# Two of five units' probabilities transposed by VectorE and GpSimd instead of TensorE, dense rows on 128 partitions, and a new order, in a two-layer recurrent-memory attention kernel

## Chip, cores, metric

One core of a Trainium2 chip runs the kernel. The metric is device microseconds of one execution, the median of three runs: 1588.75 us (1588.54 to 1590.98).

## What is computed

The input x has 2048 rows of 512. Two pairs of layers with shared weights follow each other: attention with a recurrent memory, then a dense layer, and both again.

```python
def _A_ref(x, mem0, Wq, Wk, Wv, Wo, seg_len):     # seg_len 32, M = 8 memory rows, 32 heads of 128
    mem = mem0
    for s in range(n_seg):                        # 64 segments
        h = jnp.concatenate([mem, xs], axis=1)    # 8 + 32 = 40 rows
        q, k, v = (einsum('btd,dhe->bhte', h, W) for W in (Wq, Wk, Wv))
        scores = jnp.where(mask, einsum(q, k) * scale, -1e9)
        o = einsum(softmax(scores), v)
        o = einsum('bhte,hed->btd', o, Wo)
        mem = o[:, :M, :]                         # goes into the next segment
        outs.append(o[:, M:, :])
...
x = x + _A_ref(_layernorm(x), ...)
x = x + relu(_layernorm(x) @ w1) @ w2             # 512 -> 1376 -> 512
x = x + _A_ref(_layernorm(x), ...)
x = x + relu(_layernorm(x) @ w1) @ w2
```

The memory rows make the segments of a layer a chain: segment s+1 needs the projected memory of segment s.

## The kernel before

**Steps.** Two layers run interleaved. Step k works on segment k of the first attention layer and on segment k-2 of the second (66 steps; in steps 2 to 63 both are there, "full steps"). Both segments lie side by side in HT: 2 x 40 columns, so most matmuls have 80 moving columns.

**Units.** The 32 heads form four groups p of eight. A unit is (p, xs): units 0, 1 and 2 hold eight heads each (groups 0, 1, 2), units 3 and 4 half of group 3 each. Per step and unit:

- queries_keys: 16 matmuls for four heads' q or k, copied from PSUM to qT and kT (L982 on ScalarE, L984 on VectorE).
- scores (L1133): small matmuls into one PSUM bank; rows of 40 queries at partitions 0 and 64.
- softmax: mask add (L1144), maximum (L1148), subtraction (L1151), exp on ScalarE (L1155), sum (L1158), reciprocal (L1161), multiply into P (L1175, on VectorE or GpSimd).
- turn: matmuls against the identity transpose P into PSUM (part of L726); two masked copies (L1198 on ScalarE, L1200 on VectorE) bring it to PT, one per block b of heads, with the other block's rows set to zero.
- attend (L1217): matmuls with PT as moving operand, eight per full unit, then a copy to OT.
- project: 16 matmuls for four heads (L726, st<-OT,Wo_sb), summed over all units in one PSUM bank. Project 0 is first, project 4 (16 matmuls) last. Then the memory columns go to the next step's HT.

Line 726 is the helper `across`, which issues most matmuls. Beside attention a step has the value matmuls (L1048), the dense layer of the step before, and, in steps 5 to 54, pieces of later values (vg).

**Dense layer (finish).** OX is transposed by a DMA to rows y, 64 rows of 512; add (L924), layernorm (L749, L752, L731 and L736 on GpSimd, L755), a TensorE turn of four blocks with 64 columns each ("turn da"), w1 and relu, w2 (L821), the total with x (L940, two halves), a second layernorm for the second attention layer, a turn of four blocks with 32 columns ("turn db"). GpSimd moves rows between x and Z (L909, L957, L962).

**Order.** A planner gives each engine its instructions in a fixed order. TensorE's order is a table: an operation in step k has the priority PERIOD * k + PLACE[name, phase], and TensorE takes them sorted.

```python
if PE in o.cost:
    o.prio = PERIOD * o.step + PLACE.get((o.key, phase(o.step)), -99.0)
...
first = [o for o in sorted(self.ops, key=lambda o: (o.prio, o.seq)) if PE in o.cost]
```

Phase 0 is the steady phase; phases 2 to 4 are steps 0, 1 and 2, phases 5 and 6 the last two. The other engines take what the planner's cost model has ready first, with AHEAD and the tables' priorities to choose among what is ready within LOOK. PAIRED names operations that may run as two matmuls of 64 output columns where TensorE is in that tile mode already. Buffers are rings: es has two, PT three.

Of the kernel before, what the change touches and what calls it, by code (L numbers as in the profile page):

```python
# [8 lines left out]
BF = mybir.dt.bfloat16  # L9
# [21 lines left out]
LOOK = 0.0763052  # L31
PERIOD = 26.155362
PLACE = {
    ("*turned.turng0.0", 2): -89.961, ("*turned.turng1.0", 2): -29.171, ("*turned.turng2.0", 2): -21.854,
    ("*turned.turng3.0", 2): -18.856, ("*turned.turng4.0", 2): 7.73, ("*turned.turng5.0", 2): 3.668,
    ("*turned.turng6.0", 2): 21.105, ("*turned.turng7.0", 2): 35.848, ("*values.mmg0.0", 2): -24.752,
    ("*values.mmg0.1", 2): -25.658, ("*values.mmg0.2", 2): -13.629, ("*values.mmg0.3", 2): -5.241,
    ("*values.mmg1.0", 2): -23.988, ("*values.mmg1.1", 2): -24.752, ("*values.mmg1.2", 2): -5.58,
    ("*values.mmg1.3", 2): -5.826, ("*values.mmg2.0", 2): -0.166, ("*values.mmg2.1", 2): -7.867,
    ("*values.mmg2.2", 2): -12.27, ("*values.mmg2.3", 2): -17.638, ("*values.mmg3.0", 2): -8.777,  # L40
    ("*values.mmg3.1", 2): 0.348, ("*values.mmg3.2", 2): -0.279, ("*values.mmg3.3", 2): 11.874,
    ("*values.mmg4.0", 2): 60.771, ("*values.mmg4.1", 2): 43.21, ("*values.mmg4.2", 2): 50.685,
    ("*values.mmg4.3", 2): 32.375, ("*values.mmg5.0", 2): 14.472, ("*values.mmg5.1", 2): 50.454,
    ("*values.mmg5.2", 2): 20.334, ("*values.mmg5.3", 2): 7.7, ("*values.mmg6.0", 2): 39.239,
    ("*values.mmg6.1", 2): 51.082, ("*values.mmg6.2", 2): 32.453, ("*values.mmg6.3", 2): 32.134,
    ("*values.mmg7.0", 2): 67.088, ("*values.mmg7.1", 2): 44.861, ("*values.mmg7.2", 2): 63.527,
    ("*values.mmg7.3", 2): 78.999, ("attend.mmu0.0", 0): 46.198, ("attend.mmu0.0", 2): 43.372,
    ("attend.mmu0.0", 3): 43.359, ("attend.mmu0.0", 4): 41.947, ("attend.mmu0.0", 5): 52.115,
    ("attend.mmu0.0", 6): 51.839, ("attend.mmu1.0", 0): 48.361, ("attend.mmu1.0", 2): 43.267,
    ("attend.mmu1.0", 3): 48.433, ("attend.mmu1.0", 4): 43.811, ("attend.mmu1.0", 5): 53.564,  # L50
    ("attend.mmu1.0", 6): 52.286, ("attend.mmu2.0", 0): 52.242, ("attend.mmu2.0", 2): 48.839,
    ("attend.mmu2.0", 3): 49.155, ("attend.mmu2.0", 4): 51.459, ("attend.mmu2.0", 5): 54.271,
    ("attend.mmu2.0", 6): 56.839, ("attend.mmu3.0", 0): 52.917, ("attend.mmu3.0", 2): 48.735,
    ("attend.mmu3.0", 3): 48.727, ("attend.mmu3.0", 4): 53.577, ("attend.mmu3.0", 5): 54.512,
    ("attend.mmu3.0", 6): 59.465, ("attend.mmu4.0", 0): 54.218, ("attend.mmu4.0", 2): 46.589,
    ("attend.mmu4.0", 3): 51.493, ("attend.mmu4.0", 4): 52.878, ("attend.mmu4.0", 5): 50.927,
    ("attend.mmu4.0", 6): 62.122, ("dense_layer.mm.da.0", 0): 69.095, ("dense_layer.mm.da.0", 2): 69.092,
    ("dense_layer.mm.da.0", 3): 71.014, ("dense_layer.mm.da.0", 4): 67.121, ("dense_layer.mm.da.0", 5): 78.081,
    ("dense_layer.mm.da.0", 6): 149.332, ("dense_layer.mm.da.1", 0): 69.149, ("dense_layer.mm.da.1", 2): 69.678,
    ("dense_layer.mm.da.1", 3): 72.44, ("dense_layer.mm.da.1", 4): 68.335, ("dense_layer.mm.da.1", 5): 81.881,  # L60
    ("dense_layer.mm.da.1", 6): 163.656, ("dense_layer.mm.da.2", 0): 69.921, ("dense_layer.mm.da.2", 2): 69.865,
    ("dense_layer.mm.da.2", 3): 72.468, ("dense_layer.mm.da.2", 4): 69.033, ("dense_layer.mm.da.2", 5): 78.483,
    ("dense_layer.mm.da.2", 6): 166.387, ("dense_layer.mm.da.3", 0): 72.962, ("dense_layer.mm.da.3", 2): 72.508,
    ("dense_layer.mm.da.3", 3): 75.407, ("dense_layer.mm.da.3", 4): 72.576, ("dense_layer.mm.da.3", 5): 91.676,
    ("dense_layer.mm.da.3", 6): 169.361, ("dense_layer.mm.da.4", 0): 74.146, ("dense_layer.mm.da.4", 2): 73.088,
    ("dense_layer.mm.da.4", 3): 75.634, ("dense_layer.mm.da.4", 4): 73.89, ("dense_layer.mm.da.4", 5): 96.131,
    ("dense_layer.mm.da.4", 6): 202.721, ("dense_layer.mm.da.5", 0): 74.607, ("dense_layer.mm.da.5", 2): 73.784,
    ("dense_layer.mm.da.5", 3): 76.032, ("dense_layer.mm.da.5", 4): 76.254, ("dense_layer.mm.da.5", 5): 117.834,
    ("dense_layer.mm.da.5", 6): 266.417, ("finish.turn_near.0", 6): 67.931, ("idle.spins.0", 6): 75.636,
    ("late_values.mmv0.0", 0): 55.822, ("late_values.mmv1.0", 0): 56.364, ("prepare.turns.0", 2): -92.733,  # L70
    ("project.mm.0", 0): 50.503, ("project.mm.0", 2): 48.522, ("project.mm.0", 3): 47.695,
    ("project.mm.0", 4): 46.462, ("project.mm.0", 5): 54.013, ("project.mm.0", 6): 55.445,
    ("project.mm.1", 0): 52.792, ("project.mm.1", 2): 48.552, ("project.mm.1", 3): 50.859,
    ("project.mm.1", 4): 53.188, ("project.mm.1", 5): 54.467, ("project.mm.1", 6): 56.904,
    ("project.mm.2", 0): 53.979, ("project.mm.2", 2): 51.927, ("project.mm.2", 3): 51.15,
    ("project.mm.2", 4): 54.567, ("project.mm.2", 5): 55.41, ("project.mm.2", 6): 61.468,
    ("project.mm.3", 0): 54.515, ("project.mm.3", 2): 52.343, ("project.mm.3", 3): 51.498,
    ("project.mm.3", 4): 54.73, ("project.mm.3", 5): 59.493, ("project.mm.3", 6): 62.385,
    ("project.mm.4", 0): 54.829, ("project.mm.4", 2): 52.707, ("project.mm.4", 3): 51.859,
    ("project.mm.4", 4): 55.104, ("project.mm.4", 5): 63.208, ("project.mm.4", 6): 63.808,  # L80
    ("queries_keys.mmu0.0", 0): 33.177, ("queries_keys.mmu0.0", 2): -2.267, ("queries_keys.mmu0.0", 3): 28.414,
    ("queries_keys.mmu0.0", 4): 30.223, ("queries_keys.mmu0.0", 5): 31.574, ("queries_keys.mmu0.0", 6): 40.535,
    ("queries_keys.mmu0.1", 0): 35.022, ("queries_keys.mmu0.1", 2): 10.309, ("queries_keys.mmu0.1", 3): 28.972,
    ("queries_keys.mmu0.1", 4): 29.109, ("queries_keys.mmu0.1", 5): 29.899, ("queries_keys.mmu0.1", 6): 38.292,
    ("queries_keys.mmu0.2", 0): 32.038, ("queries_keys.mmu0.2", 2): 5.691, ("queries_keys.mmu0.2", 3): 29.761,
    ("queries_keys.mmu0.2", 4): 27.054, ("queries_keys.mmu0.2", 5): 35.233, ("queries_keys.mmu0.2", 6): 41.032,
    ("queries_keys.mmu0.3", 0): 34.046, ("queries_keys.mmu0.3", 2): 8.234, ("queries_keys.mmu0.3", 3): 27.267,
    ("queries_keys.mmu0.3", 4): 27.106, ("queries_keys.mmu0.3", 5): 33.701, ("queries_keys.mmu0.3", 6): 40.622,
    ("queries_keys.mmu1.0", 0): 33.29, ("queries_keys.mmu1.0", 2): -3.555, ("queries_keys.mmu1.0", 3): 33.083,
    ("queries_keys.mmu1.0", 4): 30.633, ("queries_keys.mmu1.0", 5): 30.415, ("queries_keys.mmu1.0", 6): 41.01,  # L90
    ("queries_keys.mmu1.1", 0): 31.691, ("queries_keys.mmu1.1", 2): 7.644, ("queries_keys.mmu1.1", 3): 35.745,
    ("queries_keys.mmu1.1", 4): 27.445, ("queries_keys.mmu1.1", 5): 31.218, ("queries_keys.mmu1.1", 6): 42.927,
    ("queries_keys.mmu1.2", 0): 31.569, ("queries_keys.mmu1.2", 2): -4.781, ("queries_keys.mmu1.2", 3): 33.431,
    ("queries_keys.mmu1.2", 4): 31.298, ("queries_keys.mmu1.2", 5): 31.356, ("queries_keys.mmu1.2", 6): 40.49,
    ("queries_keys.mmu1.3", 0): 31.637, ("queries_keys.mmu1.3", 2): 9.921, ("queries_keys.mmu1.3", 3): 34.111,
    ("queries_keys.mmu1.3", 4): 29.304, ("queries_keys.mmu1.3", 5): 31.132, ("queries_keys.mmu1.3", 6): 44.867,
    ("queries_keys.mmu2.0", 0): 37.201, ("queries_keys.mmu2.0", 2): 26.988, ("queries_keys.mmu2.0", 3): 40.496,
    ("queries_keys.mmu2.0", 4): 36.639, ("queries_keys.mmu2.0", 5): 37.862, ("queries_keys.mmu2.0", 6): 46.536,
# [120 lines left out]


def t_dve(n, rate=1):
    return 0.07 + 1.042e-3 * n / rate


PART, MASKED = {ACT: 0.13, DVE: 0.10}, {ACT: 0.11, DVE: 0.065}
XBAR = 0.5, 0.2, 2.6


def t_pool(n):
    return 0.06 + 2.2e-3 * n  # L230


def t_copy(n):
    return 0.06 + 1.3e-3 * n


def phase(step):

# [1137 lines left out]
```

## Time and profile before

| what | us |
|---|---|
| median of three runs | 1588.75 |
| profiled execution, first to last instruction | 1588.6 |
| PE, PEld busy | 1569.5, 1411.1 |
| DVE, ACT, POOL busy | 1082.3, 1165.2, 314.3 |
| a full step, start to start | 23.35 to 23.8 |
| transposes of P on PE (L726, work<-ident,P), 756 of 128 and 536 of 64 output columns | 59.3 and 22.0 busy |
| masked copies to PT on ACT (320 and 160 elements) | 133.1 and 97.8 |
| masked copies to PT on DVE (320 elements) | 65.9 |

A line of the groups holds the source line, engine, operation, tiles written and read, shapes, the count, then busy time, mean time of one in ns, and the idle time ahead of it with what ended it. A line of the timeline holds the start, the length, engine, line, operation, tiles and the count that was merged. PEld is TensorE's weight load, which runs beside the matmuls; SPq is the sync engine's queue of DMA issues. The granted TensorE clock was 0.998 over the run.

### The profile page before, as it was taken

How to read it: one execution, taken by the hardware profiler on the slowest of the kernel's cores; microseconds unless marked ns; L12 is line 12 of the kernel's file. 1: busy time of each engine (PE TensorE's matmuls, PEld its weight loads, DVE VectorE, ACT ScalarE, POOL GpSimd, SP SyncE). 2: the span in 40 equal slices, each digit the busy share in tenths (PEclk: the TensorE clock that was granted, in tenths of full speed). 3: DMA queues.
4: the chain of work that ended last, by engine and by line, in shares of the span. 5: the costliest groups of instructions: out<-in, count | busy, mean ns of one | idle time of the engine just before them, and what ended most of it. 6: DMA issues, size and time to landing. Idle time of an engine off the chain costs nothing.

```text
span 1588.6 us, 100346 instructions
## 1 busy us (share of the span) xinstructions
PE 1569.5 (99%) x45458; PEld 1411.1 (89%) x45458; DVE 1082.3 (68%) x2957; ACT 1165.2 (73%) x3073; POOL 314.3 (20%) x667
## 2 busy tenths in 40 slices
PE   8999999999999999999999999999999999999998
PEld 5689999999999989999989999999998998898887
DVE  4566766766776776686676677677667667667665
ACT  4667777777777777777777777777777777777774
POOL 5112112212112212121121221211211121112110
PEclk9999999999999999999999999999999999999999
DMA  9711111111111111111111111111111111111100
GB/s 371 243 44 30 26 33 32 29 35 37 25 39 31 35 29 33 29 32 40 26 36 27 35 26 42 37 26 38 25 35 28 33 33 29 33 25 22 28 21 9
DMA packets 76540, 70.89 MB, mean 45 GB/s; under 512 B 50920, under 2 KB 62416, under 8 KB 76112
## 3 DMA queue, kind: packets, MB, share of 16 engines
q1 hardware_dynamic: 70096, 44.14, 13.1%
q0 software_dynamic: 4992, 19.40, 3.4%
q8 instruction: 356, 5.83, 1.6%
q10 hardware_dynamic: 1024, 0.93, 0.2%
q14 instruction: 72, 0.59, 0.1%
HBM read 31.53 MB, written 9.96 MB: 26 GB/s over the span
## 4 chain that ended last, share of the span: by engine, by line
PE 97%; DMA 1%; DVE 1%; POOL 1%; ACT 0%; issue 0%; DVEq 0%; POOLq 0%
PE work L726 40%; PE st L726 19%; PE fill L1048 16%; PE fill L726 8%; PE fill L821 5%; PE work L1217 5%; PE work L1133 4%; DMA xg<-in_A_x_dram 0%; DMA y<-OX 0%; DMA w_sb<-in_B_w_dram 0%; ACT HT L982 0%; POOL Wo_sb L537 0%; PE fill L711 0%; DVE ln L749 0%; POOL ln L736 0%
## 5 line engine op out<-in xcount | busy, mean ns | idle before, releaser
L726 PE MATMUL work<-HT,Wq_sb 128*128 128x80 bf16 (+2 forms) x10400 | 361.8, 201 | 3.1 <-ACT HT L982 3.1
L726 PE MATMUL work<-HT,Wk_sb 128*128 128x80 bf16 (+2 forms) x10416 | 362.7, 201 | 0.8 <-ACT HT L982 0.8
L726 PEld LDWEIGHTS <-Wq_sb 128*128 128x128 bf16 (+1 forms) x10400 | 330.9, 104 | 20.8 <-issue 6.0
L726 PE MATMUL st<-OT,Wo_sb 128*128 128x80 bf16 (+1 forms) x8448 | 345.5, 201 | 0.0
L726 PEld LDWEIGHTS <-Wk_sb 128*128 128x128 bf16 (+1 forms) x10416 | 327.1, 104 | 17.3 <-issue 2.0
L726 PEld LDWEIGHTS <-Wo_sb 128*128 128x128 bf16 x8448 | 315.7, 100 | 13.0 <-issue 12.7
L1048 PE MATMUL fill<-Wv_sb,HT 128*64 128x512 bf16 x2112 | 273.6, 381 | 1.1 <-DVE HT L984 1.0
L982 ACT CAST kT<-work 128x320 bf16<-128x320 f32 (+1 forms) x523 | 218.3, 418 | 68.6 <-PE work L726 31.1
L982 ACT CAST qT<-work 128x320 bf16<-128x320 f32 (+1 forms) x516 | 215.7, 418 | 67.5 <-PE work L726 47.2
L1198 ACT ACTIVATE PT<-work,half 128x160 bf16<-128x160 f32 (+1 forms) x515 | 231.3, 463 | 20.1 <-PE work L726 12.7
L982 ACT CAST OT<-work 128x320 bf16<-128x320 f32 (+1 forms) x461 | 186.2, 420 | 50.7 <-PE work L1217 50.6
L982 ACT CAST vw<-fill 128x512 bf16<-128x512 f32 x229 | 134.1, 586 | 113.3 <-PE fill L1048 109.8
L1144 DVE TENSOR_TENSOR es<-work,maskb 128x320 f32<-128x320 f32 (+2 forms) x330 | 136.2, 413 | 99.7 <-PE work L1133 93.2
L924 DVE TENSOR_TENSOR xg<-xg,y 64x512 f32<-64x512 f32 x65 | 44.2, 680 | 227.2 <-DMA y<-OX 226.6
L731 POOL TENSOR_SCALAR ln<-ln 32x1 f32<-32x1 f32 (+2 forms) x159 | 46.6, 293 | 566.7 <-DVE ln L752 561.0
L1155 ACT ACTIVATE es<-es 128x320 f32<-128x320 f32 (+2 forms) x330 | 136.1, 413 | 24.4 <-DVE es L1151 16.2
L1048 PEld LDWEIGHTS <-HT 128*64 128x64 bf16 x2112 | 98.9, 110 | 57.0 <-DVE HT L984 1.2
L1151 DVE TENSOR_TENSOR es<-es,mx 128x320 f32<-128x320 f32 (+2 forms) x330 | 136.3, 413 | 4.9
L1148 DVE TENSOR_REDUCE mx<-es 128x8 f32<-128x320 f32 (+2 forms) x330 | 133.9, 406 | 5.4
L1158 DVE TENSOR_REDUCE sm<-es 128x8 f32<-128x320 f32 (+2 forms) x330 | 133.4, 404 | 5.1 <-ACT es L1155 2.2
L1175 DVE TENSOR_TENSOR P<-es,sm 128x320 bf16<-128x320 f32 (+1 forms) x269 | 126.9, 472 | 3.3
L1133 PEld LDWEIGHTS <-qT 128*40 128x40 bf16 x4096 | 93.3, 97 | 35.6 <-ACT qT L982 13.6
(96 smaller groups left out, 2164.8 us busy)
## 6 DMA issues: line engine op xcount, KB each, us to landing
V<-vw SPq DMA_DIRECT2D x248, 48.0 KB
V<-vh SPq DMA_DIRECT2D x120, 64.0 KB
Wq_sb<-in_A_Wq_dram POOLq DMA_DIRECT2D x2, 2048.0 KB, 23.2
Wk_sb<-in_A_Wk_dram POOLq DMA_DIRECT2D x2, 2048.0 KB, 28.6
Wo_sb<-in_A_Wo_dram POOLq DMA_DIRECT2D x2, 2048.0 KB, 39.4
vh<-vg SPq DMA_DIRECT2D x32, 128.0 KB
xb<-in_A_x_dram SPq DMA_DIRECT2D x16, 128.0 KB
Wv_sb<-in_A_Wv_dram POOLq DMA_DIRECT2D x1, 2048.0 KB, 13.2
```

Source lines behind the costliest of these rows:

```text
L726: nc.tensor.matmul(out_[u:v, :], lhsT=lhsT[:, u:v], rhs=rhs, start=start, stop=stop, tile_position=(0, u), **more)
L821: nc.tensor.matmul(yp[64 * u:64 * u + 64, 0:256], lhsT=hT[:, fc, :], rhs=w2_sb[:, fc, 256 * u:256 * u + 256], start=(fc == 0), stop=(fc == ...
L982: nc.scalar.copy(out=out_, in_=in_)
L1048: nc.tensor.matmul(vp[64 * b:64 * b + 64, :], lhsT=cols(c4), rhs=Wv_sb[:, c4, n * 512:(n + 1) * 512], start=(c4 == 0), stop=(c4 == NC4 - 1 ...
L1133: nc.tensor.matmul(v[64 * g2:64 * g2 + L, a, i, b, :], lhsT=qT[:, hi, a * L:(a + 1) * L], rhs=kT[:, hi, a * L:(a + 1) * L], start=True, st ...
L1144: nc.vector.tensor_tensor(out=flat(es[:, A]), in0=flat(sp[:, A]), op=ALU.add, in1=maskb[:, a_lo:a_hi, :].unsqueeze(2).to_broadcast([128, n ...
L1148: nc.vector.tensor_reduce(out=mx[:, As], in_=es3(), axis=AX.X, op=ALU.max)
L1151: nc.vector.tensor_tensor(out=es3(), in0=es3(), op=ALU.subtract, in1=mx[:, As].unsqueeze(2).to_broadcast([128, ns * na, L]))
L1155: nc.scalar.activation(out=es[:, A], in_=es[:, A], func=ACTF.Exp, scale=SCALE)
L1158: nc.vector.tensor_reduce(out=sm[:, As], in_=es3(), axis=AX.X, op=ALU.add)
L1175: (nc.gpsimd if eng == POOL else nc.vector).tensor_tensor(out=o, in0=flat(es[:, A]), op=ALU.mult, in1=sm[:, As].rearrange("p (a s) -> p a ...
L1198: nc.scalar.activation(out=o, in_=i, func=ACTF.Copy, scale=half[:, b:b + 1])
```

## The change

For the groups in BLOCKED (units 0 and 1) the score matmuls are laid out with the block b on the partitions and the two heads g side by side, so that two bf16 probabilities form one 32-bit word. VectorE transposes these words in 32x32 blocks within the es tile, and GpSimd copies the blocks to PT: two copies that stay on their 64 partitions and four that move 32 partitions up or down. PT of these units is zeroed once at the start. The multiply of a blocked unit is always on VectorE, in two pieces. Units 2, 3 and 4 keep TensorE's transposes, with a ring of two (PM).

```diff
+BLOCKED = (0, 1)
...
+def t_place(n):
+    return 0.17 + 1.1e-3 * n
...
-    p_es = ring("es", 2, [128, 8 * L], F32)
-    p_PT = ring("PT", 3, [128, 2, 4, 2, L])
+    p_es = ring("es", 3, [128, 8 * L], F32)
+    p_PT, p_PM = ring("PT", len(BLOCKED), [128, 4, 2, 128]), ring("PM", 2, [128, 2, 4, 2, L])
...
+                nc.vector.tensor_tensor(out=es[:, A].rearrange("p (j k s) -> p j k s", k=L, s=2), op=ALU.add,
+                                        in0=sp[:, A].rearrange("p (j s k) -> p j k s", k=L, s=2),
+                                        in1=maskb[:, mine, :].unsqueeze(3).to_broadcast([128, nj, L, 2]))
...
+        def turn():
+            nc.vector.transpose(out=es[:, 0:64 * nj].rearrange("p (j k) -> p j k", k=64),
+                                in_=P[:, 0:512].bitcast(F32).rearrange("p (j k) -> p j k", k=64)[:, mine, :])
...
+        def stay():
+            i, o = turned_pairs()
+            for b in range(2):
+                R = slice(64 * b, 64 * b + 64)
+                nc.gpsimd.tensor_copy(out=o[R, :, b, :], in_=i[R, :, :])
+
+        def shift():
+            i, o = turned_pairs()
+            for b in range(2):
+                for c in range(2):
+                    R, T = slice(64 * b + 32 * c, 64 * b + 32 * c + 32), slice(64 * b + 32 - 32 * c, 64 * b + 64 - 32 * c)
+                    nc.gpsimd.tensor_copy(out=o[R, :, b, 32 - 32 * c:64 - 32 * c], in_=i[T, :, 32 * c:32 * c + 32])
...
+        def spread(a, i, g):
+            if p in BLOCKED:
+                return PT[:, (a - a_lo) * nx + i, :, :].rearrange("p b (q g) -> p b q g", g=2)[:, :, 0:L, g]
+            return PT[:, a, 2 * i + g, :, :]
...
-                                             rhs=PT[:, a, 2 * i + h2, :, :], start=True, stop=True, tile_position=(0, u))
+                                             rhs=spread(a, i, h2), start=True, stop=True, tile_position=(0, u))
```

The rows of the dense layer lie as two halves of 256 columns on 128 partitions (half u of a row at partition 64u), in half of the xg tiles; y, ob and xe use the other half. The layernorm takes statistics per half and swaps them between the partition halves; the turns have two blocks instead of four; the total is one instruction; a store becomes two.

```diff
+        def swap(eng):
+            for u in range(2):
+                copy_on(eng, ln[64 * u:64 * u + 64, 8:14], ln[64 - 64 * u:128 - 64 * u, 0:6])
...
-            for c4 in range(NC4):
-                across(cols, tp[:, c4 * n:(c4 + 1) * n], xn[:, c4 * 128:(c4 + 1) * 128], columns)
+            for c4 in range(blocks):
+                across(cols, tp[:, c4 * wide:(c4 + 1) * wide], xn[:, c4 * 128:(c4 + 1) * 128], columns)
...
-            for u in range(2):
-                cs = slice(256 * u, 256 * u + 256)
-                nc.vector.tensor_tensor(out=to[RB, cs], in0=x[RB, cs], in1=yp[64 * u:64 * u + 64, 0:256], op=ALU.add)
+            nc.vector.tensor_tensor(out=to[:, :], in0=x[:, :], in1=yp[:, 0:256], op=ALU.add)
...
+            for u in range(2):
+                def store(u=u):
```

PLACE, PAIRED, AHEAD and LOOK are new. Some numbers of the steady phase, before and after:

```diff
-LOOK = 0.0763052
+LOOK = 0.04480174
...
-    ("scores.mmu0.0", 0): 35.646
+    ("scores.mmu0.0", 0): 137.78
-    ("scores.mmu4.0", 0): 47.465
+    ("scores.mmu4.0", 0): 140.936
-    ("scores.turnu4.0", 0): 52.899
+    ("scores.turnu4.0", 0): 141.35
-    ("attend.mmu0.0", 0): 46.198
+    ("attend.mmu0.0", 0): 140.991
-    ("attend.mmu4.0", 0): 54.218
+    ("attend.mmu4.0", 0): 141.381
-    ("project.mm.4", 0): 54.829
+    ("project.mm.4", 0): 141.47
```

The zeroing at the start changes with the tiles: the memory rows come in through the tile of P of group 2, and the warm-up matmuls read P of group 3.

## The prediction

> **What bounds the kernel now.** I read the page first (busy time, then the chain that ended last), then TensorE's timeline over one step in the middle of the run, then VectorE's, ScalarE's and GpSimd's over the same stretch.
>
> ```profile
> span 1588.6 us, 100346 instructions
> PE 1569.5 (99%) x45458; PEld 1411.1 (89%) x45458; DVE 1082.3 (68%) x2957; ACT 1165.2 (73%) x3073; POOL 314.3 (20%) x667
> PE 97%; DMA 1%; DVE 1%; POOL 1%; ACT 0%; issue 0%; DVEq 0%; POOLq 0%
> 1259.77 4.59 PE work L726 x128
> 1283.12 4.61 PE work L726 x128
> 1306.49 4.61 PE work L726 x128
> ```
>
> TensorE is busy for 99% and makes 97% of the chain. Busy matmuls overlap, so I do not trust the 99% alone; the chain in order of time (last three lines) shows a step starting every 23.35 to 23.38 us, without drift, and TensorE's starts inside a step follow each other at 36 ns per 80 columns (32 matmuls from 808.36 to 809.50). PE's idle time is 1588.6 - 1569.5 = 19 us, and in the table of busy time by stage none of it lies between 200 and 1340 us (1140.00 of 1140.00 us busy). So a step lasts as long as its TensorE stream, and what leaves the stream leaves the time, if nothing comes late.
>
> ```profile
> 801.07 0.28 PE L726 MATMUL fill<-ident,xr 128*128 128x64 bf16 x4
> 801.19 0.74 PE L726 MATMUL work<-HT,Wq_sb 128*128 128x80 bf16 x16
> 801.76 0.45 PE L726 MATMUL work<-ident,P 128*128 128x80 bf16 x8
> 802.08 1.09 PE L726 MATMUL fill<-xnM,w_sb 128*128 128x64 bf16 x32
> 810.87 0.20 PE L1217 MATMUL work<-PT,V 128*128 128x80 bf16 x1
> 811.01 0.74 PE L726 MATMUL st<-OT,Wo_sb 128*128 128x80 bf16 x16
> 811.58 0.26 PE L726 MATMUL fill<-ident,xr 128*128 128x32 bf16 x4
> 811.69 0.73 PE L726 MATMUL st<-OT,Wo_sb 128*128 128x80 bf16 x16
> ```
>
> Read the first column, start to start: the second column holds about 0.2 us of pipeline tail.
>
> **What leaves TensorE, per step.** The eight transposes of units 0 and 1 hold it from 801.76 to 802.08: 0.32 us. The dense turn (four of 64 columns) takes 801.07 to 801.19 = 0.12 us; two of 128 columns, at 54 ns per 128 (half of the 108 ns of a 256-column matmul in this timeline), take 0.11: 0.01 saved. The second turn (four of 32 columns) takes 811.58 to 811.69 = 0.11 us; two of 64 columns at 29 ns take 0.06: 0.05 saved. Sum 0.38 us.
>
> **The new order.** TensorE's order is PLACE plus 26.155 per step, sorted, so I sorted the new numbers of the steady phase and put the durations above beside them. Both orders give the same sequence of stages and four changes of tile mode per step. The stream shrinks from 23.09 to 22.75 us (0.35; the trace's 0.38 has the gap behind the transposes in it). Counting from the start of the last output projection (project 4), before and after: scores of unit 1 at 5.62 and 5.04, of unit 0 at 8.16 and 6.72, attend of unit 0 at 16.20 and 16.03; from the scores of unit 4 to its transposes 3.98 and 4.83 us. What each stage may lose:
>
> - End of the step. Attend of unit 4 starts at 810.87, its copy runs on ScalarE from 811.21 to 811.64, project 4 starts at 811.69: 0.82 us is needed. The new order has 0.144 + 0.058 + 0.576 = 0.78 us between the two. It misses by 0.04 us a step: what is late next is this copy. Net saving 0.33 us.
> - Unit 4's softmax ended at 809.39 for a transpose at 809.50, so it was just in time. It gets 0.85 us more, and VectorE sheds work there: the total falls from two instructions (0.82 us together) to one, statistics from 512 to 256 columns (0.67 to about 0.35), against two copies of six columns (about 0.16 each, like the reciprocal of 4 columns, 0.161). Covered.
> - Units 0 and 1. Removed are four masked copies from PSUM per step (0.53 each on ScalarE or VectorE). Added are two VectorE transposes, a multiply in two pieces (some 0.25 more per unit) and twelve GpSimd copies. No row shows a VectorE transpose: 256 words lie between 0.32 (128x160) and 0.49 us (128x320) by element count; double that, 1.0, is my upper end. I take 0.45. For GpSimd the nearest rows are these:
>
> ```profile
> L998 POOL COPY HT<-xnA 128x128 bf16<-128x128 bf16 x63 | 18.4, 292 | 477.2 <-PE work L726 453.4 <-PE fill L1048 23.7
> L957 POOL COPY xg<-vx 32x512 f32<-32x512 f32 x64 | 39.0, 609 | 12.0 <-DVE vx L940 8.3
> L1175 DVE TENSOR_TENSOR P<-es,sm 128x160 bf16<-128x160 f32 x75 | 34.2, 455 | 0.2
> L1144 DVE TENSOR_TENSOR es<-work,maskb 128x160 f32<-128x160 f32 x136 | 43.7, 321 | 27.6 <-PE work L1133 21.3
> ```
>
> Between 128 and 512 elements a copy grows by 0.83 ns per element from 0.19 us, and L957 moves 32 partitions up like the new copies. So a stay copy (256 elements) costs 0.40, a shift copy (128) 0.29, and a unit 2 x 0.40 + 4 x 0.29 = 1.96 us (bounds 12 x 0.29 = 3.5 and 12 x 0.61 = 7.3 us for both units). Unit 0's scores begin at 796.53 and its P ends at 801.49, 4.96 us later; add 0.25 for the split multiply, 0.45 for the transpose and twice 0.15 for handovers (VectorE to GpSimd, 807.09 to 807.24), and GpSimd could begin 5.9 us after the scores. Unit 1 starts it at 5.04 + 5.9 = 10.9; both units are done at 10.9 + 3.9 = 14.8, or 15.1 with 0.025 of issue per copy. Attend of unit 0 comes at 16.03 plus 0.2 for mode changes, and GpSimd hands over to TensorE in 0.28 (807.69 to 807.97): some 0.9 us of cover. GpSimd is idle there (7.68 us ahead of the L998 copy at 804.74), so nothing is queued behind these copies until the dense tail at 807. VectorE does not wait for them until unit 4's mask add, which reuses unit 0's es tile at about 16.1.
> - Strided reads. Mask add, reductions and the matmuls of attend now step over every second element; no row shows this. A gain is excluded, as no element is dropped. On VectorE four instructions per unit lie between unchanged and doubled (0 to 0.4 us each), inside the same cover. On TensorE the bound is doubled columns: 16 matmuls a step by 33 ns = 0.53 us. I take nothing for both: each element still comes once, and the instructions that already read broadcast or cut patterns (L1151, the identity halves) run at the plain ones' pace.
> - Queues. SP issues one store more per step (0.34 us); its waits are for data, not for room. The row transposes halve. es rises to three buffers. All covered.
> - Ends. Half-filled steps (0, 1, 64, 65) save half each, 0.6 us in all. At the start there are bigger memsets and six more mask selects (0.2 us each) on idle engines: 0, bounds -3 to +3. At the end the chain add, statistics, total sheds about 0.8 us.
>
> **Sum.** 62 full steps x 0.33 = 20.5, plus 0.6, plus 0.8 gives 21.9 less; I allow 1.3 back for tighter places I cannot see. The span of 1588.6 goes to 1568. The profiled execution agrees with the median of the runs (1588.75) to 0.2 us, so the forecast for the time is 1568 us.
>
> **A rule against the change.** In the rows above the same multiply takes 455 ns where GpSimd copies beside it (P at 808.91 beside the copy at 808.62), against 321 for a mask add of the same size: 134 ns of waiting per meeting. Per step some six two-input VectorE instructions will meet the new copies: 6 x 0.134 = 0.8 us, just inside the 0.9 of cover, so it adds nothing to the sum. The Trainium skill (SBUF — State Buffer, Who interferes with whom) says that a VectorE instruction with two SBUF inputs and a GpSimd instruction that reads SBUF exclude each other for a whole instruction; the 134 ns agree with that in kind, and rival G is this rule at its worst.
>
> For the strided operand, the Trainium skill (SBUF — State Buffer, Door 1: The DMA port swizzle) has 16-byte lines and strides up to 8 bf16 free, by which rival D would not come; no run here shows it yet.
>
> **Rivals.**
> - A, forecast, 1568 (1562 to 1574): 0.55.
> - B, part of the gain becomes new waits at attend 0, at unit 4 or at project 4. For: the order before was already just in time in two places. At 0.2 us a step 62 x 0.2 = 12.4: 1580 (1574 to 1587): 0.20, of which 0.17 is faster by more than 0.2%.
> - C, other side: the GpSimd copies by their own length become the pace of attend 0. At 0.5 us a copy both units end at 10.9 + 6.0 = 16.9, 0.9 late; each step is 0.9 - 0.33 = 0.57 longer: 1588.6 + 62 x 0.57 = 1624. It decides from about 0.43 us a copy. For: a copy of 512 takes 0.61. Against: ours have 128 and 256. 0.09.
> - G, each of the six meetings waits for a whole copy: 6 x 0.40 = 2.4, 1.5 beyond the cover; 1588.6 + 62 x (1.5 - 0.33) = 1661. Against: the meetings seen cost 0.134. 0.03.
> - D, the strided moving operand at half pace: 62 x (0.53 - 0.33) = 12: 1601. 0.05.
> - E, start and end gain more: 1558. 0.05.
> - F, the change does not do what it says: the step is held by the loop through the memory columns, not by the stream, and stays 23.38: 1588. Against: full steps with a second late value piece last 23.79, longer by just that piece. 0.03.
>
> About 0.2% (3.2 us) is what a measurement can tell from none. Faster A + E + 0.17 = 0.77; same 0.06 (F and an edge of B); slower C + G + D = 0.17. The range 1562 to 1587 holds A and B and a little beside.
>
> **What would show it.** Right: no work<-ident,P rows for units 0 and 1, step starts every 23.05 us, PE waits still about 19 us. C: idle PE time ahead of L1217's twin, ended by POOL. D: attend matmuls of units 0 and 1 at 67 ns. B: idle before project 4, ended by ACT, or before the remaining transposes, ended by DVE. A wrong forecast would most likely be wrong in the GpSimd cover of 0.9 us.

## The result, and the profile after

The kernel after takes 1602.75 us (median of four runs, 1602.39 to 1605.17); the kernel before took 1589.87 us beside it. The ratio is 1.0086 with a 95% interval of 1.0072 to 1.01: 0.9% slower, where 1568 us had been forecast. The profiled execution after lasted 1600.7 us, 12.1 us more than the one before.

The page after, in the lines that answer to those of before (span; busy time of each engine; shares of the chain that ended last):

```profile
span 1600.7 us, 103602 instructions
...
PE 1565.4 (98%) x46325; PEld 1400.5 (87%) x46325; DVE 1089.3 (68%) x3291; ACT 1114.1 (70%) x2928; POOL 622.4 (39%) x1591
...
PE 79%; POOL 10%; DVE 5%; issue 3%; DMA 2%; ACT 1%; POOLq 0%; ACTq 0%; DVEq 0%
```

The reader is to see three things. TensorE's busy time fell, but by 4 us only, as busy time holds the 0.2 us tail of every matmul and so covers waits shorter than that. GpSimd (POOL) doubled from 314.3 to 622.4 us. And TensorE's share of the chain fell from 97% to 79%: GpSimd and VectorE now end waits on the path. Line numbers are those of the kernel after from here on: L1296 and L1303 are the stay and shift copies, L1327 attend, L743 the helper `across`, L1243 the multiply of units 2 to 4, L954 widening, L1003 carry, L748 and L753 the power of a layernorm on GpSimd, L797 its normalization.

**Where the time went.** I cut both traces at the last matmul of project 4 and added up, start to start, what each run of equal matmuls takes beyond its own pace, over 60 full steps. That splits a mean step into the stream itself and what lies between its runs (waits and changes of tile mode):

| us per step | before | after |
|---|---|---|
| mean step | 23.49 | 23.65 |
| the stream itself | 23.138 | 22.793 |
| between its runs | 0.354 | 0.857 |
| of that, ahead of the first attend of a turned unit | 0 | 0.165 |
| of that, between the last attend and turn db | 0 | 0.114 |

The stream lost 0.346 us a step, as forecast (0.35). The waits gained 0.503. The first 0.165 is one wait in 19 of the 60 steps: 13 have 0.55 to 0.59 us, three 0.72, three 0.26 to 0.41, and 14 of the 19 lie exactly four steps apart. The 0.114 is a wait of some 0.23 us in most steps. The other 0.22 is spread: 0.05 us at attend 3 for a masked copy, 0.03 for a late P of unit 3, 0.04 in other changes of tile mode, and smaller pieces.

The table of waits of TensorE after (in total, times, longest) names the first one; the second hardly shows there, since the first 0.2 us of a pause lie under the tail and count as busy:

```profile
PE work L1327 <- POOL PT L1303: 8.3, 20, 0.6
```

**The first wait, in one step without it and one with it.** GpSimd's timeline, then TensorE's first attend; first a plain step (the last matmul of the project 4 ahead of it starts at 866.69, from where I count the step):

```profile
877.27 0.99 POOL L1296 COPY PT<-es 64x256 f32<-64x256 f32 x2 [3.47 <-ACT kT L1030]
878.32 1.30 POOL L1303 COPY PT<-es 32x128 f32<-32x128 f32 x4
879.68 1.02 POOL L1296 COPY PT<-es 64x256 f32<-64x256 f32 x2
880.76 1.49 POOL L1303 COPY PT<-es 32x128 f32<-32x128 f32 x4
...
882.38 0.21 PE L1327 MATMUL work<-PT,V 128*64 128x80 bf16 x2
```

The twelve copies run from 877.27 to 882.25, and attend 0 starts at 882.38, just behind the scores ahead of it: it is in time, with nothing to spare, where the forecast had 0.9 us. Then a step that also carries the layernorm of a new group of x rows, as every fourth does (counted from 913.32), VectorE's rows for it first:

```profile
915.36 0.69 DVE L766 BATCH_NORM_STATS2 ln<-xb 128x6 f32<-128x512 bf16 x1 [2.65 <-DMA xb<-in_A_x_dram]
919.54 0.41 DVE L772 TENSOR_SCALAR xr<-xb,ln 128x512 bf16<-128x512 bf16 x1
...
924.49 1.90 POOL L1296 COPY PT<-es 64x256 f32<-64x256 f32 x4 [3.18 <-DVE es L1286]
926.44 3.10 POOL L1303 COPY PT<-es 32x128 f32<-32x128 f32 x8
...
929.60 0.23 PE L1327 MATMUL work<-PT,V 128*64 128x80 bf16 x2 [0.42 <-POOL PT L1303]
```

VectorE spends 0.41 us between two units' softmaxes on the group's rows (L772), GpSimd starts 11.17 us into the step instead of 10.58, needs 5.05 us, about as long as before, and attend 0 waits for it: its first matmul carries [0.42 <-POOL PT L1303], 0.59 us start to start. Of the 60 steps, 18 have such an L772 between the softmaxes, and all 18 wait; of the other 42 one does. No run moved this work, so the link rests on that count.

**The second wait.** GpSimd, VectorE and TensorE at the end of the plain step:

```profile
884.76 0.45 POOL L1243 TENSOR_TENSOR P<-es,sm 128x160 bf16<-128x160 f32 x1 [2.15 <-ACT PM L1265]
885.15 0.40 POOL L1008 CAST xg<-vx 128x256 bf16<-128x256 f32 x1
885.62 0.86 POOL L1003 COPY xg<-vx 32x256 f32<-32x256 f32 x2
886.53 0.83 POOL L954 CAST xg<-xb 32x256 f32<-32x256 bf16 x2
887.45 0.22 POOL L748 TENSOR_SCALAR ln<-ln 128x1 f32<-128x1 f32 x1
887.75 0.57 POOL L753 TENSOR_TENSOR ln<-ln,mhalf 128x1 f32<-128x1 f32 x1
...
886.58 0.20 DVE L794 BATCH_NORM_AGGREGATE ln<-ln 128x2 f32<-128x12 f32 x1
...
888.36 0.41 DVE L797 TENSOR_SCALAR xr<-vx,ln 128x256 bf16<-128x256 f32 x1 [0.37 <-POOL ln L753]
...
888.55 0.20 PE L1327 MATMUL work<-PM,vw 128*128 128x80 bf16 x1
888.83 0.23 PE L743 MATMUL fill<-ident,xr 128*128 128x64 bf16 x2
```

The second layernorm's variance is ready at 886.78, but its power (L748, L753) stands in GpSimd's queue behind the carry (L1003) and the widening (L954). On half rows each of the two takes two instructions (0.86 and 0.83 us). Before, they were one each (L957 and L909), and the widening stood behind the power (L731, L736):

```profile
808.62 0.61 POOL L957 COPY xg<-vx 32x512 f32<-32x512 f32 x1
809.31 0.21 POOL L731 TENSOR_SCALAR ln<-ln 32x1 f32<-32x1 f32 x1
809.61 0.56 POOL L736 TENSOR_TENSOR ln<-ln,mhalf 32x1 f32<-32x1 f32 x1
810.23 0.60 POOL L909 CAST xg<-xb 32x512 f32<-32x512 bf16 x1
```

So after, the normalized rows come at 888.77 and turn db starts at 888.83, 0.28 us after the last attend instead of 0.04.

**My theory** after this reading: the saving of TensorE is real, and the loss is GpSimd in two places, its pace at attend 0 and its queue ahead of turn db. Rivals: the new order is itself too tight; or the half rows cost by themselves; or one wait is only the other in another place.

### The profile page after: what moved, and what is told of

It reads as the page before. It is cut to its first block, busy times and chain, and to the rows that moved or that the text cites. A ratio compares the mean times of both kernels' runs of the same rounds, so it can differ in the third digit from the quotient of the medians.

```text
span 1600.7 us, 103602 instructions
## 1 busy us (share of the span) xinstructions
PE 1565.4 (98%) x46325; PEld 1400.5 (87%) x46325; DVE 1089.3 (68%) x3291; ACT 1114.1 (70%) x2928; POOL 622.4 (39%) x1591
## 4 chain that ended last, share of the span: by engine, by line
PE 79%; POOL 10%; DVE 5%; issue 3%; DMA 2%; ACT 1%; POOLq 0%; ACTq 0%; DVEq 0%
PE work L743 34%; PE fill L1096 16%; PE st L743 13%; PE fill L743 7%; PE work L1327 4%; PE work L1185 3%; PE fill L865 3%; POOL PT L1303 3%; DMA xg<-OX 2%; POOL xg L1003 1%; POOL xg L954 1%; POOL ln L753 1%; POOL PT L1296 1%; DVE xr L797 1%; POOL P L1243 1%
## 5 line engine op out<-in xcount | busy, mean ns | idle before, releaser
L743 PE MATMUL work<-HT,Wk_sb 128*64 128x80 bf16 (+2 forms) x11408 | 372.6, 201 | 0.3 <-ACT HT L1030 0.3
L743 PE MATMUL work<-HT,Wq_sb 128*128 128x80 bf16 (+2 forms) x10416 | 351.8, 201 | 4.0 <-ACT HT L1030 3.9
L743 PEld LDWEIGHTS <-Wq_sb 128*128 128x128 bf16 (+1 forms) x10416 | 328.9, 104 | 22.8 <-issue 7.5
L743 PEld LDWEIGHTS <-Wk_sb 128*64 128x64 bf16 (+1 forms) x11408 | 330.8, 106 | 16.7 <-issue 2.0
L743 PE MATMUL st<-OT,Wo_sb 128*128 128x80 bf16 (+1 forms) x8448 | 341.8, 201 | 0.0
L743 PEld LDWEIGHTS <-Wo_sb 128*128 128x128 bf16 x8448 | 313.0, 100 | 13.7 <-issue 13.1
L748 POOL TENSOR_SCALAR ln<-ln 128x1 f32<-128x1 f32 x159 | 36.8, 231 | 513.0 <-DVE ln L794 395.2
L1030 ACT CAST qT<-work 128x320 bf16<-128x320 f32 (+1 forms) x455 | 188.7, 417 | 58.4 <-PE work L743 22.1
L1296 POOL COPY PT<-es 64x256 f32<-64x256 f32 (+1 forms) x264 | 120.0, 454 | 223.9 <-ACT kT L1030 148.5
L1030 ACT CAST vw<-fill 128x512 bf16<-128x512 f32 x260 | 152.4, 586 | 60.7 <-PE fill L1096 54.8
L1030 ACT CAST OT<-work 128x320 bf16<-128x320 f32 (+1 forms) x388 | 149.2, 419 | 61.8 <-PE work L1327 61.7
L1265 ACT ACTIVATE PM<-work,half 128x160 bf16<-128x160 f32 (+2 forms) x326 | 137.4, 441 | 71.3 <-PE work L743 63.9
L1303 POOL COPY PT<-es 32x128 f32<-32x128 f32 (+1 forms) x528 | 167.7, 318 | 25.0
L753 POOL TENSOR_TENSOR ln<-ln,mhalf 128x1 f32<-128x1 f32 x161 | 110.1, 684 | 22.5 <-DVE ln L748 9.3
```

Source lines behind the costliest of these rows:

```text
L743: nc.tensor.matmul(out_[u:v, :], lhsT=lhsT[:, u:v], rhs=rhs, start=start, stop=stop, tile_position=(0, u), **more)
L753: nc.gpsimd.tensor_tensor(out=ln[R, 7:8], in0=ln[R, 7:8], in1=mhalf[R, :], op=ALU.pow)
L1030: nc.scalar.copy(out=out_, in_=in_)
L1265: nc.scalar.activation(out=o, in_=i, func=ACTF.Copy, scale=half[:, b:b + 1])
L1296: nc.gpsimd.tensor_copy(out=o[R, :, b, :], in_=i[R, :, :])
L1303: nc.gpsimd.tensor_copy(out=o[R, :, b, 32 - 32 * c:64 - 32 * c], in_=i[T, :, 32 * c:32 * c + 32])
```

## Experiments

Each is an edit of the kernel after; the diffs show its main lines, with ... where lines are left out. TensorE's order stays as written, but the planner lays out the other engines anew, and that turned out to matter. Each time is a median, with the ratio to the kernel before, run beside it, and its 95% interval.

**1. turn db later (db_late).**

```diff
-("turned.turn.db.0", 0): 167.624
+("turned.turn.db.0", 0): 167.624862     # between project 3 and project 4
```

> Edit: one number of the order table; turn db of the full steps moves behind project 3, so that 0.58 us more TensorE work lies ahead of it. Theory (turn db waits 0.23 us in most steps for a late second layernorm): the wait goes, and nothing but the copy of turn db's result is later, which nobody needs at once: 62 x 0.114 = 7 us less, about 1595.5, or less gain if the copy of attend 4, which project 4 waits for, now has 0.06 us less cover (up to 0.06 x 62 = 4 back). Rival (the time is held by the loop through the memory columns, which run through turn db): a later turn db delays the next step's queries and keys, and the time is 1602 or more.

Measured: 1594.86 us, 1.0033 (1.0023 to 1.0043), 8 us below the kernel after. The wait before turn db is gone (0.114 to 0.02 us a step), the one at attend 0 is the same (0.170). The time came out within 1 us of the theory; the loop through the memory columns does not set the pace.

**2. No shift copies (no_shift).** The eight shift copies of a step are left out.

```diff
         def shift():
-            i, o = turned_pairs()
...
+            pass
```

> Edit: the four shift copies of each turned unit are left out (so the off-diagonal 32 blocks of units 0 and 1 are never filled; this part of the computation is missing). GpSimd loses 8 copies a step, about 2.7 us. Theory (the 18 waits of 0.57 us at attend 0 are GpSimd's copies being late): they vanish, 0.165 x 62 = 10 us less, of which up to 4 may come back as the second layernorm's wait: 1593 to 1597. VectorE also meets fewer copies, which can only help. Rival (attend 0 is late by VectorE's or ScalarE's work ahead of the copies): attend 0 still waits in some 18 steps, now for the stay copies, and the time falls by less than 4 us.

Measured: 1592.07 us, 1.0011 (1.0001 to 1.002). The wait for the copies has left the table of waits, and attend 0 waits in none of the 60 steps. Before turn db the wait grew from 0.114 to 0.168 us: what was late next. The time is 1 us below the theory's range, and the fall of 10.7 us is far above the rival's 4. So attend 0 waits for the end of GpSimd's copies; how much of that is their length and how much their late start in the steps with L772, this run does not part.

**3. Both (db_noshift).** Edits 1 and 2 together; the shift copies are missing as in 2.

> Edit: turn db behind project 3, and the shift copies of units 0 and 1 left out (their off-diagonal blocks are missing). This takes both waits of the theory away at once, with nothing in their place. Theory (the two waits add up, and neither hides the other): 1592.1 without shift copies, less 0.168 us x 62 = 10.4 that this run lost before turn db: about 1582, between 1579 and 1585. What it stays above the forecast of 1568 is then neither of the two waits. Rival (one wait is only the other in another place): about 1592, as without the shift copies alone.

Measured: 1580.88 us, 0.9949 (0.9937 to 0.9962): faster than before, within 2 us of the theory. The two waits are separate and add up; without them the change wins 8.8 us. Here the stretch between the runs is 0.507 us a step, still 0.15 above before.

**4. The widening behind the power (widen_late).** The widening copies wait for the power of the second layernorm.

```diff
-plan.op(POOL, 2 * t_copy(256), widen, r=[xb], ...)
+plan.op(POOL, 2 * t_copy(256), widen, r=[xb, "powered"], ...)
-plan.op(POOL, 0.80, power, r=["half"], w=[ln])
+plan.op(POOL, 0.80, power, r=["half"], w=[ln, *done])   # done = ["powered"] for the second layernorm
```

> Edit: GpSimd's widening copies of the next step wait until the second layernorm's power has been taken, so they stand behind it in GpSimd's queue; TensorE's order is untouched. Theory (0.114 us a step before turn db come from GpSimd's queue: carry and widen, 0.86 and 0.83 us, ahead of the power): the power comes some 0.6 us earlier, the stretch between the last attend and turn db falls from 0.114 us a step to about 0, and the time falls by 62 x 0.114 = 7 us, to about 1595.5. The wait at attend 0 (0.165 us a step) stays. Rival (the new order leaves too little time for the second layernorm whatever GpSimd does, or VectorE's chain is the late one): the stretch keeps over 0.08 us and the time stays at 1602 to 1603.

Measured: 1610.27 us, 1.0126 (1.0112 to 1.014), slower than after. GpSimd and VectorE at the end of a step, and the attend behind them:

```profile
891.72 0.22 POOL L748 TENSOR_SCALAR ln<-ln 128x1 f32<-128x1 f32 x1 [0.46 <-DVE ln L794]
892.03 0.57 POOL L753 TENSOR_TENSOR ln<-ln,mhalf 128x1 f32<-128x1 f32 x1
892.66 0.83 POOL L954 CAST xg<-xb 32x256 f32<-32x256 bf16 x2
...
892.63 0.57 DVE L797 TENSOR_SCALAR xr<-vx,ln 128x256 bf16<-128x256 f32 x1 [0.82 <-POOL ln L753]
893.12 0.37 DVE L1267 TENSOR_SCALAR PM<-work,half 128x160 bf16<-128x160 f32 x1
893.55 0.20 PE L1327 MATMUL work<-PM,V 128*128 128x80 bf16 x1
```

The queue was the cause: the power now starts at once, the normalization comes 3.41 us after project 0 starts (889.22) instead of 3.94, and turn db no longer waits. But the planner, which sees the normalization earlier, put one of unit 4's masked copies (L1267) on VectorE behind it, where both were on ScalarE (L1265) before. Attend 4 now waits 0.27 us a step. The mechanism held and the time did not, outside both ranges: one wait was traded for a larger one.

**5. Both attends later (att_late).**

```diff
-("attend.mmu0.0", 0): 140.991, ("attend.mmu1.0", 0): 141.069
+("attend.mmu0.0", 0): 141.115138, ("attend.mmu1.0", 0): 141.174819
```

> Edit: two numbers of the order table; in the full steps attend 0 and attend 1 stand behind the dense layer's fifth group, which gives GpSimd's copies 0.43 us more. Theory (18 of 60 steps wait about 0.57 us at attend 0 for the last shift copy, 0.165 us a step): a wait of 0.57 falls to some 0.14, so about 0.12 us a step or 7.5 us go, unless the second layernorm's wait, which is the next late thing, takes the freed time in those 18 steps (0.23 x 18 = 4 us back): 1595 to 1599. Rival (the waits have other causes than the copies' pace, and GpSimd only follows, for instance because unit 1's softmax is paced by attend itself): the wait at attend 0 keeps its size, and the time stays within 1601 to 1604.

Measured: 1608.44 us, 1.0113 (1.0099 to 1.0127). The wait at attend 0 goes (2 waits of 0.9 us in all are left of 20). In its place the masked copies come late in nearly every step (0.24 us a step ahead of attend 2, where there was none), and turn db waits longer (0.19 against 0.11). ScalarE makes 373 of the masked copies instead of 326 and VectorE 23 instead of 70. The theory's cause held, its price did not: the time lies above both ranges. That 0.43 us of TensorE's order is not free at the next place is likely but not shown alone, as the planner also took unit 3's multiply from GpSimd here (5 of them there instead of 59).

**6. Unit 1's stay copies on ScalarE (stay_act), and with edit 1 (db_stay).**

```diff
-nc.gpsimd.tensor_copy(out=o[R, :, b, :], in_=i[R, :, :])
+(nc.scalar.copy if p == 1 else nc.gpsimd.tensor_copy)(out=o[R, :, b, :], in_=i[R, :, :])
...
```

The lines left out tell the planner of this: the transpose now claims the PT buffer, stay and shift copies wait for it and not for each other, and attend waits for both.

> Edit: the two stay copies of unit 1 go to ScalarE; GpSimd keeps unit 0's stay copies and all shift copies, and TensorE's order is untouched. GpSimd's run of twelve copies (5.0 us) loses about 1.0 us; ScalarE gains two copies of 64x256, about 0.35 us each by its 0.37 us for 128x256. Theory (attend 0 waits for GpSimd's pace, at most 0.70 us): that wait goes in all steps, 0.165 x 62 = 10 us less, up to 4 of it back as the wait before turn db, which comes as soon as attend 0 is in time: 1592 to 1597. Rival (the waits go with the whole chain through units 0 and 1, so another engine's late copy takes the place): ScalarE's evictions of queries, keys and memory columns come up to 0.7 us later, attend 0 or the scores wait for them, and the time is 1600 to 1606.

> Edit: turn db behind project 3 and unit 1's stay copies on ScalarE, both at once. Theory (two separate waits of GpSimd, 0.114 us a step before turn db and 0.165 us at attend 0, are the whole loss): both go, and as turn db is 0.58 us later the second does not come back: 1602.5 - 7 - 10 = 1585.5, between 1583 and 1589. Rival (TensorE's order is tight at so many places that the next late copy takes what is freed): 1590 to 1597.

Measured: 1612.51 us, 1.0151 (1.0137 to 1.0166), and 1604.16 us, 1.0091 (1.0076 to 1.0107). ScalarE's timeline and TensorE's scores behind it, with stay_act:

```profile
879.84 0.83 ACT L1296 COPY PT<-es 64x256 f32<-64x256 f32 x2
880.70 0.43 ACT L1030 CAST kT<-work 128x320 bf16<-128x320 f32 x1
...
881.17 0.38 PE L1185 MATMUL work<-kT,qT 128*40 128x40 bf16 x16 [0.31 <-ACT kT L1030]
```

The stay copies take 0.83 us on ScalarE, and the eviction of the next unit's keys stands behind them; scores wait for it in 47 places (15.2 us in all). The rival names the mechanism, a late eviction of keys ahead of the scores, but priced it too low (1600 to 1606): ScalarE, busy 70% of the kernel after, has no free 0.8 us there. Attend 0 no longer waits, but that gain is paid at the scores. db_stay, where theory (1583 to 1589) and rival (1590 to 1597) both missed, has the same wait at the scores in 45 places (14.7 us).

**7. TensorE's transposes back (none_new, none_old).** BLOCKED is empty; half rows are kept. none_new keeps the new order and puts the two transposes ahead of the dense layer's first group; none_old takes the four tables of before.

```diff
-BLOCKED = (0, 1)
+BLOCKED = ()
...
-ring("PM", 2, [128, 2, 4, 2, L])
+ring("PM", 3, [128, 2, 4, 2, L])
...
```

> Edit: no unit is turned by VectorE and GpSimd; units 0 and 1 are transposed by TensorE again, in the new order (their two transposes just ahead of the dense layer's first group), with the dense rows as half rows kept. TensorE's stream gets 0.32 us a step back. Theory (the new order is not the loss, the GpSimd copies are): attend 0 does not wait; the wait before turn db may stay at 0.1 to 0.2: a step is 22.79 + 0.32 + 0.36 + 0.1 to 0.2 = 23.57 to 23.67, as long as now; about 1597 to 1604. Rival (the new order is itself too tight for masked copies on ScalarE and VectorE, 16 us of waits in 62 steps are its own): 1602 + 20 = 1620 or more.

> Edit: no unit is turned by VectorE and GpSimd, and the order is that of before; only the dense rows as 128 half rows are left of the change (with the three es buffers). Theory: TensorE's stream loses 0.06 us a step (turn da 0.01, turn db 0.05), VectorE sheds work, and GpSimd's carry and widen grow by 0.25 us each; in the order of before the second layernorm's power stood ahead of widen. 62 x 0.06 = 4 us less, plus up to 0.8 at the end: about 1585, between 1583 and 1590. Rival (the half rows cost by themselves, through the swap of statistics on ScalarE and VectorE and the carry in two pieces ahead of the power): turn db waits 0.1 to 0.25 us a step, 1590 to 1600.

Measured: 1667.33 us, 1.0491 (1.0476 to 1.0505), and 1599.36 us, 1.0061 (1.0049 to 1.0074). Both times lie on the rivals' side, but by other waits than the rivals had named. With none_new nothing waits for GpSimd, but unit 3's transposes wait 1.04 us a step for VectorE's P:

```profile
PE work L743 <- DVE P L1243: 55.5, 61, 2.4
```

GpSimd makes none of the multiplies there; after, it made 59, one a step. With none_old nothing waits before turn db; the largest new wait is 0.115 us a step at unit 4's P, and in the step that I read a copy of OT stands ahead of that unit's sum on VectorE. So the new order, as the planner fills it, does not fit TensorE's transposes, and the half rows do not fit the old order as they stand; neither run says what a refitted order would give. What the half rows would cost in an order made for them alone stays open.

**8. The order of the attends (db_swap, db_swap2, db_swap2_pin).** VectorE and GpSimd finish unit 1 first, while TensorE takes attend 0 first. db_swap exchanges the two numbers of attend 0 and 1 and has edit 1; db_swap2 also puts attend 0 behind the dense layer's fourth group; db_swap2_pin is db_swap2 with each multiply fixed to the engine that it has in the kernel after, by 9 us added to the other engine's cost.

```diff
-("attend.mmu0.0", 0): 140.991, ("attend.mmu1.0", 0): 141.069
+("attend.mmu0.0", 0): 141.069, ("attend.mmu1.0", 0): 140.991       # db_swap
+("attend.mmu0.0", 0): 141.115138                                    # db_swap2, between da.3 and da.4
```

> Edit: three numbers of the order table; turn db behind project 3, and attend 1 ahead of attend 0, as GpSimd finishes unit 1 first. An attend takes 0.29 us of TensorE, so the unit that GpSimd finishes last gets that much more; no engine gets more work. Theory (18 of 60 steps wait some 0.57 us for unit 0's last shift copy): each such wait falls by 0.29, 18 x 0.29 = 5.2 us less than with turn db alone (1594.9): about 1589.5, between 1587 and 1592. Rival (TensorE's order is tight at the next place, the masked copies ahead of attend 2 to 4, as when both attends were moved by 0.43 us): nothing gained, 1594 to 1598.

> Edit: as the swap, and attend 0 stands one group of the dense layer later (behind the fourth instead of ahead of it), some 0.2 us more. Theory: the waits of 0.57 us fall by 0.29 + 0.2 to about 0.1, 18 x 0.47 = 8.5 us less than with turn db alone: about 1586, between 1583 and 1590, which would be faster than before by 0.2%. Rival: attend 0's two copies on ScalarE come 0.2 us later and push the masked copies that attend 2 to 4 wait for: 0.1 to 0.2 us in every step, 1590 to 1600.

> Edit: as the run with attend 0 one group later (1647), but unit 3's multiply is fixed to GpSimd and the other units' to VectorE, as the kernel after has them; there the planner had moved that multiply from GpSimd to VectorE in every step (2 on GpSimd instead of 59), and unit 4's transposes waited 1.1 us for VectorE. Theory (the 1.1 us come from that move alone; a later attend 0 costs nothing by itself): the wait for unit 4 goes, 1647 - 62 x 1.1 = 1579 at the least, and with unit 3's P later by one reduction, up to 0.3 us a step back: 1583 to 1598. Rival (attend 0 later by 0.2 us is itself what delays unit 4, through its evictions): 1630 or more.

Measured, db_swap: 1592.01 us, 1.0012 (1.0003 to 1.0021). The wait at the last-finished unit fell from 0.170 to 0.09 us a step, as the theory said; 0.03 of it came back ahead of unit 3's transposes. It is the fastest variant of the change here that computes everything, and it does not beat the kernel before.

db_swap2: 1647.22 us, 1.036 (1.0346 to 1.0374). Neither theory. The wait for GpSimd is gone (0.7 us in all), but unit 3's transposes wait 1.1 us for P in every step, as in none_new (the last expectation above names unit 4 there, a slip: it is unit 3). The groups of the multiplies on GpSimd, first db_swap, then db_swap2:

```profile
L1243 POOL TENSOR_TENSOR P<-es,sm 128x160 bf16<-128x160 f32 (+1 forms) x59 | 26.6, 451 | 119.6 <-ACT PM L1265 87.5 <-DVE sm L1227 26.6 <-PE work L743 3.0
```

```profile
L1243 POOL TENSOR_TENSOR P<-es,sm 128x160 bf16<-128x160 f32 (+1 forms) x2 | 0.8, 385 | 4.3 <-PE work L743 2.7 <-DVE sm L1227 1.6
```

A shift of 0.2 us in TensorE's table made the planner move one multiply a step from GpSimd to VectorE. In the step that I read, VectorE takes the reciprocal for it at 908.77 and the multiply only at 910.00, behind the second layernorm's statistics (L787), another reciprocal and the swap of statistics (L1032); the transposes start at 910.47.

db_swap2_pin, meant to show that this move alone costs the time: 1867.15 us, 1.1749 (1.1732 to 1.1765). The theory (1583 to 1598) fell, and the number on the rival's side (1630 or more) is not by the rival's evictions. GpSimd's timeline, then TensorE's:

```profile
912.63 0.40 POOL L1008 CAST xg<-vx 128x256 bf16<-128x256 f32 x1 [2.54 <-DVE vx L985]
913.10 0.86 POOL L1003 COPY xg<-vx 32x256 f32<-32x256 f32 x2
914.01 0.83 POOL L954 CAST xg<-xb 32x256 f32<-32x256 bf16 x2
914.92 0.22 POOL L748 TENSOR_SCALAR ln<-ln 128x1 f32<-128x1 f32 x1
915.23 0.57 POOL L753 TENSOR_TENSOR ln<-ln,mhalf 128x1 f32<-128x1 f32 x1
915.76 0.45 POOL L1243 TENSOR_TENSOR P<-es,sm 128x160 bf16<-128x160 f32 x1
...
916.27 0.31 PE L743 MATMUL work<-ident,P 128*128 128x80 bf16 x2 [3.04 <-POOL P L1243]
```

The multiply is on GpSimd again, but now at the end of the dense tail's queue instead of at its head, and unit 3's transposes wait 3.1 us for it. That is the second wait of the kernel after in large: what costs is not GpSimd's work but what stands ahead of an urgent instruction in its queue. Whether a later attend 0 costs anything by itself was not shown, as both runs were ruled by the multiply.

## Why the prediction was wrong, step by step

- **TensorE's stream: right.** 0.346 us a step left it (0.35 forecast). The 0.04 us expected back at project 4 did not come, which was luck for the sum: 0.35 less 0.04 is 0.31, not the 0.33 that it used, 1 us a run.
- **VectorE's transpose: right.** 0.44 us (0.45 taken), though no row of a transpose stood behind the choice.
- **Strided reads: right.** A matmul of attend from PT, with 64 output columns, starts every 18.1 to 18.8 ns, where it was 17.9 to 18.0 before: 3% or 0.02 us a step, far from rival D's doubling. Mask add and subtraction of blocked units take 0.49 us like the others. The Trainium skill's rule (SBUF — State Buffer, Door 1: The DMA port swizzle), by which such strides are free, agrees but for these 3%, whose cause is not shown.
- **The cover at attend 0: the step that failed.** The "some 0.9 us of cover" was 0.1 in a plain step and below zero in the 18 steps with L772. It is the fault that the prediction itself held most likely. Three terms had been mis-sized, all in the same direction. The copies' own lengths were right (0.39 and 0.28 us, 0.40 and 0.29 taken), but without a neighbour they start every 0.454 and 0.328 us, which makes 4 x 0.454 + 8 x 0.328 = 4.44 us instead of 3.9 + 0.3. The meetings with VectorE, priced at 0.8 us and then left out as "just inside the 0.9 of cover", add 5.0 - 4.44 = 0.5 us; cover can be spent once, and here two small terms spent it. And GpSimd's beginning 5.9 us after the scores was read in one plain step (its terms add up to 5.96, and it is 5.97 after); in a step with a new group of rows it is 6.56. One term erred the other way: the 0.28 from GpSimd to TensorE was no handover, as project 0 kept TensorE busy until 808.00; where TensorE waits it is 0.06 (929.54 to 929.60). Rival C put its point of decision at 0.43 us a copy; the mean was 5.0/12 = 0.415, so C's mechanism and its sign, idle time ahead of attend ended by POOL, came in the steps with the extra VectorE work.
- **GpSimd's dense tail: not in the sum.** That "nothing is queued behind these copies until the dense tail" was true, but the tail was itself changed, and only VectorE's part of it was priced. Carry and widening became two instructions each, and the new order left the power behind them: 0.114 us a step, 8 us by db_late.
- **Ends.** The end was forecast 0.8 us shorter; the last two steps and what follows came out 0.75 us longer. Steps 0 to 2 are 2.1 us longer (step 2 takes 27.11 instead of 24.77). Their cause stays open.
- **Rival B was the right kind and too small.** It had new waits of 0.2 us a step, at attend 0 but not at turn db; the two named here make 0.28, and all of them 0.50. Of the 34.7 us between forecast and result, the two waits are about 17 (0.279 x 62), the smaller waits 14 and the ends 3.
- **What db_noshift leaves.** The forecast saving is 1588.75 - 1568 = 20.7 us, that run's 8.8. Of the 12 us between, the stretches between runs take 0.507 - 0.354 = 0.15 us a step, 9.5 us over 62 steps, in small pieces: 0.03 from turn db to project 4, 0.02 at late rows, 0.04 in mode changes, the rest smaller. Most of what remains is the longer ends.
- **The rule on the shared port.** The prediction set the Trainium skill (SBUF — State Buffer, Who interferes with whom) beside 134 ns a meeting. After a stay copy beside a blocked multiply, a VectorE instruction with two inputs, the next copy starts 0.59 us later instead of 0.454, so again about 0.14; beside a subtraction 0.64. That agrees with the rule in kind; a whole VectorE instruction (0.49 us) per meeting is not what these copies show, and rival G (1661) did not come.

## What to carry to other kernels

Cover is one budget: add issue spacing, meetings with other engines and the steps with extra work before you compare it with the slack, and take the slack from the worst step of the cycle, not from one. When work moves to an idle engine, list that engine's whole queue up to its next urgent instruction, as a short instruction that others wait for costs what stands ahead of it. In a kernel whose order a planner lays out, an edit of one number moves work between engines elsewhere, so read where each instruction went before you read the time.

## What I had not expected of the hardware

- GpSimd's copies are spaced wider than they last: 64x256 f32 lasts 0.39 us and repeats after 0.454, 32x128 lasts 0.28 and repeats after 0.328.
- TensorE's granted clock fell in the waits of db_swap2_pin. One step by stretch (last columns: granted clock, DMA share, GB/s): full clock, the wait of 3.0 us, half clock, full clock again.

```profile
911.50:913.00 1.50, 1.50 (x46) 1.30 (x40) 1.50 (x7) 1.18 (x4) 0.37 (x1) 1.00 0.00 0
913.20:916.20 3.00, 0.03 (x1) 0.00 (x0) 1.37 (x5) 0.00 (x0) 2.69 (x7) 0.84 0.06 11
916.30:918.00 1.70, 1.70 (x27) 1.70 (x28) 0.55 (x2) 1.01 (x3) 0.00 (x0) 0.50 0.05 10
920.00:922.00 2.00, 2.00 (x34) 2.00 (x32) 0.25 (x1) 0.15 (x1) 0.00 (x0) 0.50 0.00 0
924.00:930.00 6.00, 6.00 (x183) 5.34 (x181) 2.58 (x7) 4.38 (x12) 0.89 (x2) 1.00 0.08 16
```

In stretches of 0.5 us it falls to a half some 2.0 us after the last matmul and is full again 5.8 us after the next. In that time 32 matmuls of project take 2.13 us start to start instead of 1.16. Between start and end of the run the half clock comes 55 times, for 3.41 us (40 times) or 6.83 (15 times, as here, 915.26 to 922.08). The mean full step, 28.07 us, is 4.6 us longer than that of db_swap (23.48), for a wait of 3.1. In db_swap2, with waits of 1.1 us in every step, the mean granted clock stayed at 0.998. The Trainium skill (TensorE: Matmul & The Clock Gate, What's actually happening) has the half clock after an idle window of some 3.4 us, in windows that run freely, and the full one after as long a busy one; the lengths of one or two such windows agree, while a wait of 3.0 us was enough here.
